# Five PSUM banks for scores and two for transposes in the first batch of attention, instead of four and three

## The chip, the cores and the metric

The kernel runs on one core of one Trainium2 chip. The metric is the device time of one execution in microseconds; the kernel before takes 909.62 us (median of three runs, 909.54 to 909.81).

## The reference

Three layers follow each other. Block-causal attention over 4 batches, 8 heads, 576 positions and 64 channels, in blocks of 64; a feed-forward layer with a squared ReLU; and a mixture of eight experts, of which every token takes one.

```
scores = scale * np.matmul(q, k.transpose(0, 1, 3, 2))
scores = np.where(block_i >= block_j, scores, -1000000000.0)
attn = np.exp(scores - scores.max(-1)); attn = attn / (attn.sum(-1) + 1e-09)
x = np.matmul(attn, v)                     # 2304 tokens x 512
h = np.maximum(x @ w_in, 0.0); x = (s * (h * h) + b) @ w_out
e_idx = np.argmax(x @ w_gate + modality_bias[modality_id], axis=1)
out[mask] = gate_w[mask, None] * (np.maximum(x[mask] @ w1[e], 0.0) @ w2[e])
```

## The kernel before

**Units and steps.** Attention takes two heads at once, a pair, so that 128 partitions are full: four pairs in a batch, sixteen pairs in all. A pair has nine steps, one for each block of 64 query rows; step i has (i + 1) * 64 columns of scores, and the last step is done in two parts of 288 columns. A step passes through these stages (lines of the profile in brackets):

- scores: matmuls into a bank of the pool `sc` [L144 for steps 0 and 1; L147 for the others, three matmuls each, since q and k are split into a high and a low part];
- the row maximum on VectorE (DVE) [L149, and L152 to join the two parts of the last step], then the exponential on ScalarE (ACT), which reads the bank of scores and writes a buffer `p` in SBUF [L154]. The bank of scores is free after it;
- the reciprocal of the row sum on DVE [L163 to L166] and the scaling of p on GpSimd (POOL) [L167];
- the transposes of p on TensorE (PE) into a bank of the pool `tp` [L186], and the copy of that bank to SBUF on ACT [L192], after which the bank is free and so is the buffer p, of which there are six;
- p times v on PE, once for steps 0 to 3 and once for steps 4 to 8, into the bank `o` [L210], copied to `x` by ACT [L212].

**The next pair's q and k.** While a pair is in its steps 4 to 6, q and k of the next pair are turned: four transposes of q into a bank `tw` [L94], which ACT reads four times [L103, L106] and DVE twice for the low part `ql` [L87]; four of k into another bank `tw`, read by ACT twice [L118, L119] and by DVE once [L89, `kl`]; and one for the last 64 rows of both into a bank `te` [L124], read by ACT three times and DVE three times. These banks are of the same pool as those of the p transposes. I call the stretch from the second p times v of one pair to the first exponential of the next pair a pair's boundary; the first batch, with the first step of the second, has three of them, named A, B and C here.

**Banks.** PSUM has eight banks in this kernel. A pool gives out its banks in turn, and a tile waits until all readers of the tile that had its bank before are done. In the first batch (steps 0 to 36 of the program) the pools are `BANKS_0`: scores, transposes, o. After it, `early.close()` and `BANKS_A = (3, 2, 1)`, since the feed-forward layer then takes two banks for work that runs beside attention.

```
LAGS = (1, 5, 7)
NPBUF = 6
BANKS_0 = (4, 3, 1)
BANKS_A = (3, 2, 1)
        if step == per:
            early.close()
            banks.open(c2, tc, 1, *BANKS_A)
```

**What sets the order.** The code is written step by step, with the lags of `LAGS` between a step's stages; a list scheduler in the framework then orders each engine's instructions by its own estimate of when operands and banks are free. So the number of banks also changes the order in which each engine's instructions stand in the program. From step 8 on, weights of the feed-forward layer are converted from 64-bit to 32-bit numbers beside attention [L338 to L340 on DVE, L373 on ACT, L344 on POOL]. The transfers stand in SP's queue [L76, L77 for q, k and v; L329 for the weights].

Of the kernel before, what the change touches and what calls it, by code (L numbers as in the profile page):

```python
# [280 lines left out]
LAGS = (1, 5, 7)  # L281
NPBUF = 6
PTBUF = 1
BANKS_0 = (4, 3, 1)
P_COPY = lambda nc, i: nc.scalar.copy


# [991 lines left out]
def kernel(  # L1279
# [33 lines left out]
    with ExitStack() as c2, ExitStack() as early:  # L1313
        pieces = ffn.beside(c2, range(begun))
        banks = Banks()
        banks.open(early, tc, 0, *BANKS_0)
        plan = [blk for blk in range(begun) for _ in range(NA[blk] + 3)]
# [72 lines left out]
```

## Time and profile before

| | |
|---|---|
| median of three runs | 909.62 us |
| profiled execution, its own time | 911.51 us |
| its span, first to last instruction | 909.9 us |
| mean granted clock of TensorE | 0.992 |
| busy: PE, DVE, ACT, POOL | 878.7, 642.1, 570.0, 218.5 us |

The span's first 62 to 65 us hold the first batch of attention. A matmul's row shows when it started and how long it took until its result was written; since matmuls overlap, a busy PE is not one at its peak. An engine runs its instructions in the program's order, so one that waits holds up all that stand behind it. In a row of the timeline, what stands in square brackets is the idle time of that engine just before the row and who ended it.

### The profile page before, as it was taken

The numbers are of one execution on the slowest core, as the hardware profiler recorded it, in microseconds if no ns is written. First come the engines' busy times: TensorE is split into PE (matmuls) and PEld (weight loads), VectorE is DVE, ScalarE is ACT, GpSimd is POOL, SyncE is SP. The second block draws the span as 40 slices with busy tenths as digits, with TensorE's granted clock in tenths as the row PEclk, the third lists the DMA queues.
The fourth block names the chain that finished last, engine by engine and source line by source line (L and its number), as shares of the span: only waits on it lengthen the run. The fifth ranks groups of instructions, "written<-read, shape, count | busy, mean of one in ns | idle before, by whom it ended". The sixth has DMA issues, their size and how long they took to land. (4 is left out here: it accounts for less than half of the span.)

```text
span 909.9 us, 17059 instructions
## 1 busy us (share of the span) xinstructions
PE 878.7 (97%) x5765; PEld 727.5 (80%) x5765; DVE 642.1 (71%) x1490; ACT 570.0 (63%) x1165; POOL 218.5 (24%) x335
## 2 busy tenths in 40 slices
PE   6889999999999999999999999999999999999996
PEld 5667778888879789999999999998477776776775
DVE  4888996473646445878967777767688887776783
ACT  5888786585757553333565555542287777776773
POOL 4577566133324200000000000002024322222110
PEclk9999999999999999999999999999999999999999
DMA  5666553322221132545212212115345696637500
GB/s 149 162 166 176 148 139 79 98 53 77 62 85 30 49 118 93 162 139 174 59 47 63 76 61 60 47 47 194 110 163 213 230 383 248 223 128 255 189 23 29
DMA packets 109481, 113.84 MB, mean 125 GB/s; under 512 B 62679, under 2 KB 80617, under 8 KB 109387
## 3 DMA queue, kind: packets, MB, share of 16 engines
q1 hardware_dynamic: 105579, 100.74, 35.2%
q0 software_dynamic: 3808, 11.94, 3.8%
q8 instruction: 48, 0.79, 0.4%
q14 instruction: 46, 0.38, 0.1%
HBM read 143.58 MB, written 19.80 MB: 180 GB/s over the span
## 5 line engine op out<-in xcount | busy, mean ns | idle before, releaser
L387 PE MATMUL ph<-xh,wih 128*128 128x256 f32 x576 | 165.7, 288 | 0.1
L387 PE MATMUL ph<-xh,wil 128*128 128x256 f32 x576 | 162.4, 282 | 0.0
L387 PE MATMUL ph<-xl,wih 128*128 128x256 f32 x576 | 162.2, 282 | 0.0
L167 POOL TENSOR_TENSOR p<-p,rc 128x64 f32<-128x64 f32 (+2 forms) x144 | 111.9, 784 | 125.4 <-DVE rc L166 71.4
L387 PEld LDWEIGHTS ph<-xh,wih 128*128 128x128 f32 x576 | 109.1, 189 | 5.2 <-issue 2.9
L387 PEld LDWEIGHTS ph<-xl,wih 128*128 128x128 f32 x576 | 109.2, 190 | 1.3 <-issue 0.2
L387 PEld LDWEIGHTS ph<-xh,wil 128*128 128x128 f32 x576 | 109.2, 190 | 0.6 <-issue 0.4
L149 DVE TENSOR_REDUCE nm<-sc 128x1 f32<-128x288 f32 (+8 forms) x160 | 70.8, 449 | 54.8 <-PE sc L147 47.4
L154 ACT ACTIVATE p<-sc,nm 128x288 f32<-128x288 f32 (+8 forms) x160 | 80.8, 508 | 20.6 <-DVE nm L149 8.7
L1014 DVE TENSOR_TENSOR w1l<-raw,w1h 128x1024 fp32r<-128x1024 f32 x60 | 71.7, 1222 | 22.9 <-ACT w1h L1013 18.7
L1014 DVE TENSOR_TENSOR w2l<-raw,w2h 128x1024 fp32r<-128x1024 f32 x64 | 75.4, 1219 | 10.8 <-ACT w2h L1013 10.6
L1022 POOL DMA_INDIRECT xr<-x_d,gidx_e x2 | 2.3, 1132 | 310.6 <-PE ph L387 310.3
L186 PE MATMUL tp<-ident,p 128*128 128x128 f32 x400 | 66.2, 282 | 5.8 <-POOL p L167 2.5
L1013 ACT CAST w2h<-raw 128x1024 fp32r<-128x1024 f32 x64 | 66.0, 1049 | 7.6 <-PE py L1117 7.1
L397 ACT ACTIVATE r<-ph 128x512 f32<-128x512 f32 x44 | 26.4, 599 | 68.2 <-PE ph L387 68.1
L1013 ACT CAST w1h<-raw 128x1024 fp32r<-128x1024 f32 x60 | 61.6, 1050 | 9.4 <-PE ph L1100 8.7
L192 ACT COPY pt<-tp 128x512 f32<-128x512 f32 (+3 forms) x128 | 61.6, 502 | 7.5 <-PE tp L186 7.0
L398 DVE SCALAR_TENSOR_TENSOR r<-r,sc 128x512 f32<-128x512 f32 x44 | 36.2, 823 | 40.6 <-ACT r L397 40.3
L186 PEld LDWEIGHTS tp<-ident,p 128*128 128x128 f32 x400 | 46.4, 143 | 17.5 <-POOL p L167 6.4
L1117 PE MATMUL py<-w2h,hh 128*128 128x512 f32 x128 | 52.2, 408 | 0.0
L210 PE MATMUL o<-pt,raw_v 128*64 128x320 f32 (+4 forms) x448 | 51.0, 367 | 0.0
L1117 PE MATMUL py<-w2h,hl 128*128 128x512 f32 x128 | 50.8, 397 | 0.0
(306 smaller groups left out, 2272.9 us busy)
## 6 DMA issues: line engine op xcount, KB each, us to landing
raw<-in_moe_w_dram SPq DMA_DIRECT2D x172, 512.0 KB
xr<-xT_d SPq DMA_DIRECT2D x19, 512.0 KB
wr<-in_moe_w_in_dram SPq DMA_DIRECT2D x16, 512.0 KB
wr<-in_moe_w_out_dram SPq DMA_DIRECT2D x16, 512.0 KB
row<-part_d SPq DMA_DIRECT2D x20, 256.0 KB
x_d<-row SPq DMA_DIRECT2D x18, 256.5 KB
xT_d<-x SPq DMA_DIRECT2D x16, 288.0 KB
raw_q<-in_q_dram SPq DMA_DIRECT2D x32, 128.0 KB
```

Of the source, the lines that this page charges most:

```text
L149: ps.last["max"] = nc.vector.tensor_reduce(nm[:, e:e + 1], sc[:, 0:w], AX.X, ALU.max, negate=True)
L154: ps.last["exp"] = nc.scalar.activation(pr[:, k0:k0 + w], scs[e][:, 0:w], AF.Exp, bias=nm[:, 0:1], accum_out=sm[:, e:e + 1])
L167: ps.last["scale"] = nc.gpsimd.tensor_mul(pr[:, 0:n], pr[:, 0:n], rc.to_broadcast([P, n]))
L186: nc.tensor.transpose(t[:, e * P:(e + 1) * P], st[u][i][0][:, c * P:(c + 1) * P], ident)
L192: P_COPY(nc, i0)(o, src)
L210: nc.tensor.matmul(o[r, first * D:n], vt[:, c, hh], p[:, first:, c, r], start=(c == 0), stop=(c == cs[-1]))
L387: nc.tensor.matmul(ph[:, e], self.wi[p][w][:, c, e * P:(e + 1) * P], x[a][:, c], start=(n == 0), stop=(n == 3 * KC - 1))
L397: nc.scalar.activation(r, ph.rearrange("p e (t n) -> p (e t) n", n=P), AF.Relu)
L398: nc.vector.scalar_tensor_tensor(r, r, self.sc[:, 0:1], r, ALU.mult, ALU.mult)
L1013: self.nc.scalar.copy(ws[0][c], r)
L1014: self.nc.vector.tensor_sub(ws[1][c], r, ws[0][c].bitcast(F32))
L1117: nc.tensor.matmul(py, hT[a][:, c], self.w2s[w][c // 2][:, c % 2 * D:c % 2 * D + D], start=(t == 0), stop=(t == 3 * KF - 1))
```

## The change

In the first batch the pool of scores has five banks instead of four and that of transposes two instead of three. Nothing else in the text of the kernel changes.

```
-BANKS_0 = (4, 3, 1)
+BANKS_0 = (5, 2, 1)
```

The scheduler orders the first batch anew; from the second step of the second batch on, the engines' orders agree again. The following pieces are of the program's order, without times. On PE at the start of the program, with the first pair's scores, before the change (the pair in work is the one with kh_171, the next one's q and k are raw_q_207 and raw_k_212):

```order
L144 MATMUL sc_203<-kf_173,qf0_140 128x128
L147 MATMUL sc_224<-kh_171,qh0_136 128x256
L147 MATMUL sc_237<-kh_171,qh0_136 128x256
L94 MATMUL tw_262<-ident_60,raw_q_207 128x128 x4
L147 MATMUL sc_224<-kl_172,qh0_136 128x256
L147 MATMUL sc_224<-kh_171,ql0_138 128x256
L147 MATMUL sc_237<-kl_172,qh0_136 128x256
L147 MATMUL sc_237<-kh_171,ql0_138 128x256
L94 MATMUL tw_289<-ident_60,raw_k_212 128x128 x4
```

And with the change, at the same place:

```order
L144 MATMUL sc_203<-kf_173,qf0_140 128x128
L147 MATMUL sc_224<-kh_171,qh0_136 128x256
L147 MATMUL sc_237<-kh_171,qh0_136 128x256
L147 MATMUL sc_256<-kh_171,qh0_136 128x320
L124 MATMUL te_181<-ident_60,raw_t_149 128x128
L147 MATMUL sc_224<-kl_172,qh0_136 128x256
L147 MATMUL sc_224<-kh_171,ql0_138 128x256
L147 MATMUL sc_237<-kl_172,qh0_136 128x256
L147 MATMUL sc_237<-kh_171,ql0_138 128x256
L147 MATMUL sc_256<-kl_172,qh0_136 128x320
L147 MATMUL sc_256<-kh_171,ql0_138 128x320
L94 MATMUL tw_262<-ident_60,raw_q_207 128x128 x4
```

The next pair's q is now turned after the scores of step 4 instead of before the second matmul of step 2's; a fifth score tile (sc_256) is opened early, and the first pair's tail transposes (te_181) have moved behind it.

On PE at boundary A, before the change (o_554 is the first pair's second p times v, tw_488 and tw_515 are the third pair's q and k, tp_528 the second pair's first p transposes):

```order
L94 MATMUL tw_488<-ident_60,raw_q_337 128x128 x4
L147 MATMUL sc_536<-kh_286,ql1_144 128x448
L147 MATMUL sc_570<-kh_286,qh1_142 128x512
L210 MATMUL o_554<-pt1_383,raw_v_157 64x320 x6
L210 MATMUL o_554<-pt1_383,raw_v_157 64x192 x2
L210 MATMUL o_554<-pt1_383,raw_v_157 64x64 x2
L94 MATMUL tw_515<-ident_60,raw_k_342 128x128 x4
L186 MATMUL tp_528<-ident_60,p_389 128x128
L186 MATMUL tp_528<-ident_60,p_406 128x128
L124 MATMUL te_542<-ident_60,raw_t_338 128x128
```

With the change:

```order
L147 MATMUL sc_570<-kh_286,qh1_142 128x512
L210 MATMUL o_554<-pt1_383,raw_v_157 64x320 x6
L210 MATMUL o_554<-pt1_383,raw_v_157 64x192 x2
L210 MATMUL o_554<-pt1_383,raw_v_157 64x64 x2
L94 MATMUL tw_488<-ident_60,raw_q_337 128x128 x4
L94 MATMUL tw_515<-ident_60,raw_k_342 128x128 x4
L147 MATMUL sc_570<-kl_287,qh1_142 128x512
L147 MATMUL sc_570<-kh_286,ql1_144 128x512
L147 MATMUL sc_608<-kh_286,qh1_142 128x288
L147 MATMUL sc_608<-kl_287,qh1_142 128x288
L147 MATMUL sc_608<-kh_286,ql1_144 128x288
```

The transposes of q have moved from before the p times v to behind it, and those of p (tp_528) from right behind k to behind all scores of the pair's last step and the first of the next pair's (four rows further down, not shown). Boundaries B and C have the same move.

On ACT at boundary A, before the change:

```order
L212 COPY x_417<-o_554 128x320
L118 COPY kf_514<-tw_515 128x128
L119 CAST kh_512<-tw_515 128x512
L192 COPY pt0_527<-tp_528 128x2x128
L154 ACTIVATE p_532,sm_535<-sc_536,nm_534 128x448
```

With the change:

```order
L106 ACTIVATE qh0_136<-tw_488 64x6x64
L118 COPY kf_514<-tw_515 128x128
L119 CAST kh_512<-tw_515 128x512
L154 ACTIVATE p_532,sm_535<-sc_536,nm_534 128x448
L192 COPY pt0_527<-tp_528 128x2x128
```

The reads of the turned q now stand between the copy of o and the reads of the turned k; before they stood ahead of the copy of o. The exponential of step 6 (128x448) needs the buffer p of six steps before, so it waits for the transposes tp_528 in either order.

## Rows read from the trace of the kernel before

**Rows 1.** The page: busy time of each engine; PE's busy tenths in 40 slices.

```profile
PE 878.7 (97%) x5765; PEld 727.5 (80%) x5765; DVE 642.1 (71%) x1490; ACT 570.0 (63%) x1165; POOL 218.5 (24%) x335
PE   6889999999999999999999999999999999999996
```

**Rows 2.** Stretches: length, busy PE, PEld, DVE, ACT, POOL, clock, DMA share, GB/s.

```profile
22.09:36.79 14.70, 12.51 (x93) 9.60 (x92) 12.16 (x41) 13.29 (x46) 7.21 (x16) 1.00 0.79 180
36.79:51.05 14.26, 13.58 (x91) 10.53 (x90) 12.42 (x43) 12.06 (x42) 10.95 (x18) 0.88 0.62 179
51.05:65.10 14.05, 10.71 (x78) 8.11 (x76) 12.43 (x41) 12.30 (x42) 10.23 (x18) 1.00 0.62 160
65.10:81.81 16.71, 15.18 (x100) 11.45 (x102) 13.60 (x43) 13.94 (x46) 10.61 (x19) 0.90 0.57 155
```

**Rows 3.** Timeline of PE and ACT, boundaries A and C: start, us, what.

```profile
26.78 2.28 PE L210 MATMUL o<-pt,raw_v 128*64 128x320 f32 x20
...
56.43 2.28 PE L210 MATMUL o<-pt,raw_v 128*64 128x320 f32 x20
...
27.29 0.47 ACT L106 ACTIVATE qh<-tw 64x384 fp32r<-64x384 f32 x1
...
30.58 0.66 ACT L154 ACTIVATE p<-sc,nm 128x448 f32<-128x448 f32 x1
...
60.24 0.66 ACT L154 ACTIVATE p<-sc,nm 128x448 f32<-128x448 f32 x1
```

**Rows 4.** Timeline of PE, ACT and DVE, 86 to 94 us, banks (3, 2, 1).

```profile
86.65 2.28 PE L210 MATMUL o<-pt,raw_v 128*64 128x320 f32 x20
...
88.97 0.43 ACT L212 COPY x<-o 128x320 f32<-128x320 f32 x1 [0.57 <-PE o L210]
89.55 0.27 ACT L103 ACTIVATE qf<-tw 64x128 f32<-64x128 f32 x1 [0.15 <-PE tw L94]
...
90.38 0.47 ACT L106 ACTIVATE qh<-tw 64x384 fp32r<-64x384 f32 x1
...
92.89 0.64 ACT L154 ACTIVATE p<-sc,nm 128x448 f32<-128x448 f32 x1 [1.25 <-PE tp L186]
...
90.68 0.69 DVE L149 TENSOR_REDUCE nm<-sc 128x1 f32<-128x512 f32 x1 [0.54 <-PE sc L147]
91.29 1.11 DVE L87 SCALAR_TENSOR_TENSOR ql<-tw,qh 64x384 fp32r<-64x384 f32 x2
```

**Rows 5.** Timeline of ACT: last copies before the o of A and C.

```profile
25.16 0.82 ACT L192 COPY pt<-tp 128x512 f32<-128x512 f32 x2
...
54.92 0.76 ACT L192 COPY pt<-tp 128x512 f32<-128x512 f32 x2 [0.17 <-PE tp L186]
```

**Rows 6.** Timeline of DVE and PE, the first pair.

```profile
8.05 0.69 DVE L89 TENSOR_TENSOR kl<-tw,kh 128x512 fp32r<-128x512 f32 x1
...
10.03 1.09 PE L94 MATMUL tw<-ident,raw_q 128*128 128x128 f32 x4 [0.97 <-DMA raw_q<-in_q_dram]
10.77 0.56 PE L147 MATMUL sc<-kl,qh 128*128 128x256 f32 x1
```

**Rows 7.** Behind boundary A: PE and ACT timeline, and a stretch as in rows 2.

```profile
36.46 0.38 PE L147 MATMUL sc<-kh,qh 128*128 128x256 f32 x1 [1.49 <-ACT p L154]
...
40.99 0.76 ACT L192 COPY pt<-tp 128x512 f32<-128x512 f32 x2 [1.16 <-PE tp L186]
...
38.40:42.00 3.60, 3.58 (x16) 3.06 (x16) 3.04 (x10) 2.01 (x7) 3.60 (x4) 0.53 0.16 46
```

**Rows 8.** Behind boundary C: the same views.

```profile
64.13 0.50 ACT L154 ACTIVATE p<-sc,nm 128x288 f32<-128x288 f32 x1 [0.87 <-DVE rc L166]
...
65.56 0.74 PE L144 MATMUL sc<-kf,qf 128*128 128x128 f32 x2 [2.48 <-ACT p L154]
...
65.50:69.00 3.50, 3.44 (x16) 2.51 (x17) 1.90 (x9) 1.87 (x7) 2.17 (x2) 0.52 0.38 112
```

**Rows 9.** Timeline of ACT behind boundary A.

```profile
35.82 0.50 ACT L154 ACTIVATE p<-sc,nm 128x288 f32<-128x288 f32 x1 [0.23 <-DVE rc L165]
```

## The prediction

> **What bounds the kernel now.** I read the page first, then stretches of the first batch, then the timelines of PE, ACT and DVE there. PE is busy 878.7 of 909.9 us, and from the fourth slice of the page's strip to the last but one every slice reads 9 [rows 1]: behind the first batch there is hardly a gap in which a microsecond lost or won early could vanish. The engines' orders agree again from the second batch on, so I carry what the first batch loses or wins to the end one for one.
>
> Inside the first batch PE alone is not the bound. Three stretches run from the first exponential of one pair to that of the next, 14.70, 14.26 and 14.05 us [rows 2]. ACT is busy 13.29, 12.06 and 12.30 of them, which leaves 1.41, 2.20 and 1.75 us; PE is the busier one in the second, where its clock stands at 0.88. So a pair is a chain over PE, ACT and DVE with ACT nearest to full: what makes ACT wait, and is not made up by a wait that ACT would have had anyway, lengthens the pair.
>
> **The change part by part.** It adds, removes and lengthens no instruction. It moves them, and changes who waits for a bank.
>
> *The boundaries (loss).* With three transpose banks the scheduler turns the next pair's q before the second p times v, and ACT reads it while PE does these 20 matmuls: the last read of q starts at 27.29 under the matmuls of 26.78 + 2.28 [rows 3]. With two banks both are held by the last p transposes until their copies are made, so q comes behind the p times v, the new order on PE says. Then a chain stands open: p times v, copy of o, four reads of q on ACT, two `ql` on DVE, and only then is a bank free for the next p transposes, for which the step-6 exponential waits because it needs their buffer p. Queued behind that exponential on ACT are the copy of those transposes, the tail's reads and all further exponentials.
>
> The trace of before has this very order once, where the banks are (3, 2, 1) [rows 4]: p times v starts at 86.65, copy of o at 88.97, q from 89.55 to 90.85, `ql` from 91.29, and the exponential at 92.89 after a wait of 1.25 us: 6.24 us from start to exponential. Boundaries A and C have 30.58 - 26.78 = 3.80 and 60.24 - 56.43 = 3.81 [rows 3]. The difference is 2.43 us. Of it 0.44 is a row maximum that held DVE until 91.29 while q was ready at 90.85 [rows 4], and need not stand there: 1.99 to 2.43.
>
> Against it, p times v can start sooner, since the transposes of q no longer stand ahead of it: its last operand is copied at 25.16 + 0.82 = 25.98 and 54.92 + 0.76 = 55.68, and it started 0.80 and 0.75 us later [rows 3, 5]. The gain is 0 to 0.80; I take 0.75, as the new order has only score matmuls there. Net per boundary: 1.99 - 0.80 = 1.2 at least, 2.43 at most; I take (1.99 + 2.43) / 2 - 0.75 = 1.45. What covers some of it: at C ACT waited 0.87 us for DVE before the last step's exponential [rows 8], at A 0.23 [rows 9]; a later ACT finds that work done. A, B, C: 1.22 + 1.45 + 0.58 = 3.25 us. The ends are 3 x 1.2 - 1.1 = 2.5 and 3 x 2.43 - 1.1 = 6.2.
>
> *The first pair (gain).* Before, PE stood 0.97 us at the transposes of the second pair's q, whose transfer landed late, and scores that could use `kl` from 8.05 + 0.69 = 8.74 on started at 10.77 [rows 6]. Now scores come first and q is turned when it is there. The gain is at least 0 (ACT and DVE may set the pace) and at most 10.77 - 8.74 = 2.03; I take the wait itself, 0.97.
>
> *The fifth score bank (gain).* Behind boundary A PE waited 1.49 us for a bank of scores that an exponential had to free, and then ran 3.6 us at a granted clock of 0.53, near the lower level of 1.2 GHz; ACT waited 1.16 us there for the slow transposes [rows 7]. With five banks this score tile takes the bank of the step before, so this wait goes. At most that gives 1.49 and half of 3.58, together 3.3 us; at least nothing, if the clock falls there again. What is late next is the bank of transposes, and PE's idle time at the boundary grows. I take half of ACT's own wait, 0.6.
>
> *The clock at B (loss).* Both low spells, 0.53 and 0.52, come behind a standstill of PE of 1.49 and 2.48 us [rows 7, 8]; the boundary B has neither now. With the chain above PE stands still at B too. The cost is 0 to half of 3.58, 1.8 us; as ACT sets most of the pace I take 0.6.
>
> *At no cost:* at the change of pools the first tile of the new score pool waits, in either order, for the same exponential, so the wait of 2.48 us [rows 8] stays; the moved tail transposes lie in it. On SP one or two transfers of weights pass those of q, which is turned later by the length of the p times v.
>
> Sum: 3.25 - 0.97 - 0.6 + 0.6 = +2.3 us. On the profiled execution's own time of 911.51 this is 913.8 (span 909.9 to 912.2). The median of the runs is 1.89 below that execution, so the forecast is 909.62 + 2.3 = 911.9 us.
>
> **The rivals.** *The fifth bank wins (faster).* If PE's scores, not ACT's chain, set the pace, the first pair gives its 2.03 and boundary A its 3.3, 5.3 in all, against boundaries at their lower end, 2.5: -2.8 us, 906.8 us. The point from which it decides is a boundary that costs under 5.3 / 3 = 1.8 us each together with gains at their upper ends. For it: PE did wait for score banks, 1.49 and 2.48 us. Against it: the longer of these two stays, and ACT is busy 85 to 90% of a pair.
>
> *They cancel (no change).* With the boundaries at 2.5 and the gains at 0.97 and ACT's full 1.16, no new spell at B: +0.4, 910.0 us. For it: the pair behind the change of pools, with only two transpose banks, took 16.71 us, but with ACT idle for only 2.77 of it and a clock of 0.90 in it [rows 2], so two banks need not cost much in themselves.
>
> *The clock falls at every boundary (slower still).* Each standstill brings a spell at half clock, and boundary A is not relieved: 3.25 - 0.97 + 1.8 = +4.1, 913.7 us. For it: both longest waits of PE in these stretches were followed by one. Against it: behind the first standstill it took 1.9 us of normal running before the clock fell, so not each need bring one. The Trainium skill bears on this (TensorE: Matmul & The Clock Gate, section A second HAM failure mode: psum-queue depth-cycling): where groups of matmuls go round through few PSUM banks, PE idles shortly between them, its clock swings between the levels, and throughput is lost although single matmuls look normal. By that rule the time is this rival's; the two spells of rows 7 and 8 agree with it, the stretch from 51.05 to 65.10 with clock 1.00 shows no case of it.
>
> **How the numbers follow.** What a measurement of this kernel can tell from no change is 0.2%, 1.8 us. I give the forecast 0.40, the half clock at every boundary 0.18, cancelling 0.28 and the faster rival 0.14. So slower by over 0.2% is 0.58, within 0.2% is 0.28, faster 0.14. The boundary term decides: it has a row of this kernel for its size, while the gains are waits that may turn into others. The range for 8 in 10 is 908.4 to 914.8: it leaves out most of the faster rival, and reaches past the half-clock rival by 1.1 us because the boundary may cost up to 2.43 each. The forecast's own range is 911.4 to 913.2.
>
> **What would show it.** Right, if in the changed profile the step-6 exponential stands 5.2 to 6.3 us behind the start of the second p times v at A, B and C with a wait for `tp` just ahead of it; if PE's wait of 0.97 for raw_q and that of 1.49 for a score bank are gone; if a stretch with a clock near 0.5 stands behind B; and if the first exponential of the fifth pair, 65.10 before, comes at about 67.4. Wrong, if that exponential comes at or before 65.1: then the boundaries cost less than I took, or ACT's waits elsewhere shrank more. Also wrong, if it is late and the end is not: then the rest of the program has slack that I deny it.

## The result and the profile after

With five banks for scores and two for transposes the kernel takes 915.60 us (median of four runs, 915.12 to 916.16), against 909.61 us before in the same job: a ratio of 1.0063, with a 95% interval of 1.0050 to 1.0075. It is slower by 6.0 us by the medians. The forecast was 911.9, with a range up to 914.8: the direction was right, and the size was less than half of what came. The profiled execution of after took 916.16 us (span 914.5, mean granted clock 0.986); that of before 911.51 (span 909.9, clock 0.992), so the two traces differ by 4.65 us.

The page of after: busy time of each engine, and in 40 slices PE's busy tenths and the granted clock in tenths [rows 1].

```profile
PE 882.9 (97%) x5765; PEld 730.7 (80%) x5765; DVE 639.9 (70%) x1490; ACT 570.5 (62%) x1165; POOL 218.5 (24%) x335
...
PE   6978999999999999999999999999999999999996
...
PEclk9988999999999999999999999999999999999999
```

Counts are unchanged, PE is busy 4.2 us longer, and the third and fourth slice (46 to 91 us) show a clock below 9 tenths, where before had 9 in every slice.

The first exponential of the second, the fourth and the fifth pair, from the timeline of ACT (start, us, what):

```profile
20.71 0.36 ACT L154 ACTIVATE p<-sc,nm 128x64 f32<-128x64 f32 x1
...
52.78 0.36 ACT L154 ACTIVATE p<-sc,nm 128x64 f32<-128x64 f32 x1
...
69.75 0.36 ACT L154 ACTIVATE p<-sc,nm 128x64 f32<-128x64 f32 x1
```

And the stretches from one to the next, with columns as in [rows 2]; the second begins at the third pair's, 37.87:

```profile
20.71:37.87 17.16, 15.41 (x108) 11.70 (x105) 12.79 (x44) 12.64 (x43) 8.54 (x17) 0.94 0.78 201
37.87:52.78 14.91, 12.08 (x79) 8.98 (x79) 12.28 (x43) 12.31 (x43) 8.74 (x15) 0.91 0.58 153
52.78:69.75 16.97, 14.60 (x88) 11.32 (x84) 11.60 (x41) 12.79 (x42) 10.79 (x18) 0.80 0.47 126
```

Before they took 14.70, 14.26 and 14.05 us. After starts 1.38 us ahead (20.71 against 22.09) and then loses 2.46, 0.65 and 2.92 us. At the fifth pair, forecast for 67.4, it is 69.75 - 65.10 = 4.65 us late, and the span ends 4.6 us late: between these two traces, what the first batch lost went to the end one for one. The clock column, 0.94, 0.91 and 0.80 instead of 1.00, 0.88 and 1.00, is the part that the prediction had too small.

The boundaries A and B in the timelines of PE, ACT and DVE (columns as in [rows 3, 4]):

```profile
26.39 2.28 PE L210 MATMUL o<-pt,raw_v 128*64 128x320 f32 x20
...
32.05 0.41 PE L186 MATMUL tp<-ident,p 128*128 128x128 f32 x2 [0.68 <-DVE ql L87]
...
28.71 0.43 ACT L212 COPY x<-o 128x320 f32<-128x320 f32 x1 [0.72 <-PE o L210]
29.29 0.27 ACT L103 ACTIVATE qf<-tw 64x128 f32<-64x128 f32 x1 [0.15 <-PE tw L94]
...
32.39 0.64 ACT L154 ACTIVATE p<-sc,nm 128x448 f32<-128x448 f32 x1 [1.02 <-PE tp L186]
...
30.79 1.11 DVE L87 SCALAR_TENSOR_TENSOR ql<-tw,qh 64x384 fp32r<-64x384 f32 x2
...
42.50 2.27 PE L210 MATMUL o<-pt,raw_v 128*64 128x320 f32 x20
...
47.05 0.43 PE L144 MATMUL sc<-kf,qf 128*128 128x64 f32 x2 [0.85 <-ACT kf L118]
48.01 0.41 PE L186 MATMUL tp<-ident,p 128*128 128x128 f32 x2 [0.53 <-DVE ql L87]
...
52.22 1.55 PE L210 MATMUL o<-pt,raw_v 128*64 128x256 f32 x8
```

This is the chain as forecast: p times v at 26.39, copy of o at 28.71, q read from 29.29 on, `ql` until 31.90, the transposes at 32.05 and the exponential at 32.39, 6.00 us behind the start. At B it is 48.34 - 42.50 = 5.84, at C 65.84 - 59.99 = 5.85. The last row is the new thing: at B the next p times v of eight matmuls takes 1.55 us; at full clock, behind A at 35.67, it takes 0.87.

### The profile page after: what moved, and what is told of

Same layout as the page of the kernel before. It is cut to its first block, busy times and chain, and to the rows that moved or that the text cites. A ratio compares the mean times of both kernels' runs of the same rounds, so it can differ in the third digit from the quotient of the medians.

```text
span 914.5 us, 17060 instructions
## 1 busy us (share of the span) xinstructions
PE 882.9 (97%) x5765; PEld 730.7 (80%) x5765; DVE 639.9 (70%) x1490; ACT 570.5 (62%) x1165; POOL 218.5 (24%) x335
## 5 line engine op out<-in xcount | busy, mean ns | idle before, releaser
L186 PE MATMUL tp<-ident,p 128*128 128x128 f32 x400 | 68.4, 289 | 7.5 <-DVE ql L87 2.5
L1117 PE MATMUL py<-w2h,hl 128*128 128x512 f32 x128 | 50.8, 397 | 0.0
```

The lines of the kernel that those rows point to most:

```text
L186: nc.tensor.transpose(t[:, e * P:(e + 1) * P], st[u][i][0][:, c * P:(c + 1) * P], ident)
L1117: nc.tensor.matmul(py, hT[a][:, c], self.w2s[w][c // 2][:, c % 2 * D:c % 2 * D + D], start=(t == 0), stop=(t == 3 * KF - 1))
```

## The experiments

The theories. **Theory 1:** the loss comes from the lost third transpose bank, which puts the next pair's q behind p times v; **1a:** its price is the chain over ACT up to the step-6 exponential. **Theory 2:** its price is rather the half clock that follows PE's standstills. **Theory 3:** the fifth score bank or the new order costs by itself. A stretch at about half the granted clock is called a spell below. Each kernel was run 5 to 12 times, beside the kernel before in the same job (medians of before 909.59, 910.34 and 909.60 us in the jobs of e1 to e4, e5 to e8 and e9 to e12), and each ratio is against before of its own job.

**Two transpose banks alone (e1_421).**

```
-BANKS_0 = (5, 2, 1)
+BANKS_0 = (4, 2, 1)
```

> Two banks for transposes as in the changed kernel, but four for scores as before; the eighth bank lies idle. Theory 1 (the third transpose bank is what is lost: q is turned behind p times v, the step-6 exponential comes 5.8 to 6.0 us behind its start, and PE's standstills there bring spells at half clock): as slow as the changed kernel or slower, 914 to 917 us. Theory 3 (the fifth score bank and the earlier scores that it allows are what costs): as before, 909 to 911 us.

Measured: 914.92 us, ratio 1.0069 (1.0052 to 1.0087). Theory 1 holds; at A the exponential stands 6.24 us behind p times v, a little more than expected. In its trace the fifth pair's first exponential is at 69.69, against 69.75 with five score banks: the fifth bank gives nothing, and costs nothing, that these figures show.

**Eight buffers p, with the change and without it (e2_521_p8, e3_431_p8).**

```
-NPBUF = 6
+NPBUF = 8
```

> The changed kernel with eight buffers p instead of six, so that the step-6 exponential needs no transposes of six steps before. Theory 1a (the chain over ACT to that exponential is the main cost, 1.0 us of wait in each of four places): 3 to 4 us are won back, 911.5 to 912.5 us, and the clock spells shrink since scores' banks come free sooner. Theory 2 (the half clock behind each boundary is the main cost, and it hangs on PE's standstills for kf and ql, which stay): at most 2 us are won, 913.5 to 915.5 us, with stretches of granted clock near 0.5 behind the same boundaries.

> Control: the kernel before with eight buffers p. Its step-6 exponentials come 3.8 us behind the second p times v and wait little, so all theories give 908.5 to 910.5 us.

Measured: 907.72 us, ratio 0.9983 (0.9968 to 0.9998), with banks (5, 2, 1); 907.70 us, ratio 0.9984 (0.9973 to 0.9995), with (4, 3, 1). Both sizes were missed: the control won 1.9 us too, and with the change 7.9 us came back, twice what theory 1a gave. But the comparison is clear: with eight buffers the two splits of the banks take the same time, within intervals of 1.0 to 1.4 us either way. ACT at boundary A of e2_521_p8:

```profile
25.88 0.63 ACT L154 ACTIVATE p<-sc,nm 128x448 f32<-128x448 f32 x1
...
27.19 0.43 ACT L212 COPY x<-o 128x320 f32<-128x320 f32 x1 [0.59 <-PE o L210]
...
31.23 0.37 ACT L192 COPY pt<-tp 128x256 f32<-128x256 f32 x1 [0.19 <-PE tp L186]
```

q still stands behind p times v (24.87), but the step-6 exponential now runs under it, at 25.88 instead of 6 us behind. The granted clock of this trace is 1.00 in all of the first batch. So with eight buffers the new order costs nothing in the total. Inside the first batch it still costs something. From the second pair's first exponential to the fifth's, with banks (5, 2, 1) and then with (4, 3, 1), columns as in [rows 2]:

```profile
20.56:64.42 43.86, 36.88 (x260) 27.37 (x258) 36.98 (x123) 38.01 (x125) 28.14 (x50) 1.00 0.69 181
```

```profile
22.00:63.93 41.93, 34.81 (x257) 26.86 (x255) 36.65 (x124) 37.31 (x124) 28.03 (x50) 1.00 0.73 185
```

Both are at full clock, and the new order is 1.93 us longer; its start, 1.44 us earlier, hides most of that. The traces of after and of this kernel end 10.0 us apart (914.5 and 904.5), of which 69.75 - 64.42 = 5.3 lie in the first batch. The rest lies behind it, where the control gained too.

**A bank for q alone (e4_q_bank).** Line 94 takes its bank for q from a pool of its own.

```
-BANKS_0 = (5, 2, 1)
+BANKS_0 = (4, 2, 1)
+        if ph == 0:
+            self.f = ctx.enter_context(tc.tile_pool(name="a0_ps_f", bufs=1, space=PSUM, reuse_waits="tile"))
-        t = ps.t.tile([P, 512], F32, name="tw", tag="t")
+        pool = ps.f if own and ps.f else ps.t
+        t = pool.tile([P, 512], F32, name="tw", tag="t")
```

> Four banks for scores, two for transposes, and the eighth bank for the next pair's turned q alone. Theory 1 (what is lost is q turned ahead of p times v): the order of before comes back at the boundaries, the step-6 exponential 3.8 to 4.5 us behind the start of p times v, 908.5 to 911 us. Rival (it is the transposes of p themselves that need three banks): 913 us or more, with ACT waits for tp in the middle of pairs.

Measured: 906.52 us, ratio 0.9967 (0.9955 to 0.9978); faster than expected, and than both kernels. The exponential stands 3.80 us behind p times v at A, B and C. Two banks are enough for p, k and the tails, if q has one that these don't hold.

**q one step earlier (e5_521_q_early).**

```
-                    if i == 4:
+                    if i == (3 if u < 4 else 4):
```

> The changed kernel (banks 5, 2, 1; six buffers p), with the next pair's q turned one step earlier in the first batch, so that the program's order has it ahead of the second p times v again. Theory 1 (the loss is q turned behind p times v, which opens the chain to the step-6 exponential): at least two thirds of the 6 us come back, 908 to 911.5 us, the exponential 4 to 4.8 us behind the start of p times v, and no spell at half clock behind B. Rival (two banks for transposes are too few by themselves, whatever the order): 914 to 916 us.

Measured: 909.80 us, ratio 0.9995 (0.9983 to 1.0007): all of the loss is gone with the banks still at (5, 2, 1). Boundary B in the timelines of PE and ACT:

```profile
41.78 2.16 PE L210 MATMUL o<-pt,raw_v 128*64 128x320 f32 x16 [0.48 <-ACT pt L192]
...
39.97 0.49 ACT L106 ACTIVATE qh<-tw 64x384 fp32r<-64x384 f32 x1
...
45.85 0.68 ACT L154 ACTIVATE p<-sc,nm 128x448 f32<-128x448 f32 x1
```

q is read at 39.97, before p times v, and the exponential comes 4.07 us behind it, without a wait. This is the cleanest test of theory 1, and its rival fell. No spell stands behind B (1.00 from 45 to 55 us); one stands behind A instead (0.72 from 32 to 38 us), so the earlier q does not remove every spell.

**Repeated matmuls in PE's standstill (e6_521_fill4, e7_521_fill8, e10_521_fill3), beside the changed kernel once more (e9_521_again).** The step-0 score matmul of the four boundaries is done 5, 9 and 4 times; the order of all other rows is unchanged.

```
-                scored[0] = nc.tensor.matmul(
+                for _ in range(5 if i == 0 and u in (1, 2, 3, 4) else 1): scored[0] = nc.tensor.matmul(
```

> The changed kernel, whose step-0 score matmuls are done five times instead of once at the four boundaries (same result, no new wait, order of all engines unchanged otherwise), so that TensorE works in part of its wait for ql. Theory 2 (the half clock that follows these standstills is the larger part of the loss): the spells shrink or go, and the time falls by 2 to 4 us, to 911.5 to 913.5 us. Theory 1a (the chain over ACT is the larger part, the half clock lies under ACT's waits): 914.5 to 916.5 us even where the clock stays up.

> The same with nine of these matmuls instead of one, which covers the whole wait for ql (0.5 to 0.7 us) and may overrun it by some tenths at each boundary. Theory 2: as or below the kernel with five, 911 to 913.5 us, and no stretch near half clock behind A, B or C. Theory 1a: 915 to 917.5 us.

> The changed kernel once more, beside the one with repeated matmuls on the same chip, to size what the repeats win. All theories: 914.5 to 916.5 us.

> The changed kernel with the step-0 score matmuls of the four boundaries done four times, in the same order. If the spells of half clock behind the first pair's boundary and behind B stay away as with five, the time is 1.7 us (by medians of two jobs) to 3.4 us (by the first batch of two traces) below the changed kernel of this job; if four are too few, the spells are back and it is within 0.5 us of it.

Measured: 913.91 us (ratio 1.0044, 1.0031 to 1.0057) with five, 914.00 us (1.0046, 1.0032 to 1.0060) with nine; in another job 913.30 us (1.0039, 1.0026 to 1.0052) with four and 913.71 us (1.0043, 1.0028 to 1.0058; runs from 911.98 to 916.03) for the unchanged after, less than I had expected. With five, in stretches of columns as in [rows 2]:

```profile
16.00:24.00 8.00, 7.07 (x55) 5.89 (x55) 5.90 (x27) 6.69 (x25) 5.49 (x12) 1.00 0.67 184
46.00:54.00 8.00, 6.93 (x52) 5.75 (x53) 6.34 (x25) 6.93 (x24) 5.15 (x10) 1.00 0.75 172
```

And the exponential at its boundary B, from the timeline of ACT:

```profile
47.46 0.63 ACT L154 ACTIVATE p<-sc,nm 128x448 f32<-128x448 f32 x1 [1.05 <-PE tp L186]
```

The spells behind the first pair's boundary and behind B are gone in this trace, while the chain is whole: 47.46 - 41.43 = 6.03 us. Its fifth pair begins at 66.34, so between this trace and that of after the spells make 69.75 - 66.34 = 3.4 us. The trace with four is a closer match to after: the same start (20.70), the same chain (6.01, 5.84 and 5.84 us), a clock of 1.00 from there to 62 us, and the fifth pair at 65.64, which makes the spells 4.1 us:

```profile
20.70:65.64 44.94, 39.73 (x280) 30.75 (x279) 37.04 (x126) 37.47 (x123) 27.98 (x50) 0.97 0.67 178
```

The medians don't confirm this size. The repeats win 1.7 us against the first job and 0.4 us beside after on one chip, which the intervals can't tell from nothing. So the expectation for four failed: the spells stayed away in the execution that left a trace, but the median is not 1.7 to 3.4 us lower; the eight executions range from 911.60 to 915.82 us, with clocks of 0.992 down to 0.987. Nine matmuls, also at 1.00 from the second pair to the fifth, came out between the two theories' ranges. They took 2.22 us, not some tenths more than the wait but 0.9, which I had mis-sized; they lengthen the chain to 6.93 us.

The unchanged after was thus 1.9 us faster in the later job. The times of its eleven executions go with the clock: the four with a mean of 0.990 or 0.991 took 911.98 to 913.71 us, the seven with 0.984 to 0.988 took 915.12 to 916.16. All four of the first job were of the latter. So luck has a part in the miss: the later job's 913.71 lies inside the forecast's range, the first job's 915.60 outside it. Before shows the same on a smaller scale: of 62 executions in the three jobs, the 35 at 0.992 have a median of 910.60, the 12 at 0.996 one of 908.82 us.

**Seven buffers p (e11_521_p7).** NPBUF = 7, banks (5, 2, 1).

> The changed kernel with seven buffers p. Now the exponential of step 7, not of step 6, needs the buffer that the first p transposes of the pair free; it comes about half a microsecond of ACT work later. Theory 1a: ACT has the step-6 exponential to do under p times v, its wait for tp falls from 1.0 to below 0.6 us per boundary, and 3 us or more come back: 909 to 912.5 us. Rival (what helped with eight buffers was something else, in the later batches, where the control with banks 4, 3, 1 won 1.9 us too): 913 us or more.

Measured: 910.58 us, ratio 1.0007 (0.9998 to 1.0016). ACT's waits, from the second pair's first exponential to the fifth's (us in total, times, longest), of after and then of this kernel:

```profile
ACT x L212 <- PE o L210: 3.7, 4, 1.5
ACT pt L192 <- PE tp L186: 3.5, 3, 1.5
ACT p L154 <- PE tp L186: 2.7, 3, 1.0
```

```profile
ACT p L154 <- PE tp L186: 2.6, 3, 0.9
...
ACT x L212 <- issue: 1.0, 1, 1.0
ACT x L212 <- PE o L210: 0.5, 2, 0.4
...
ACT pt L192 <- PE tp L186: 0.2, 1, 0.2
```

The time came as theory 1a had it, but not by the wait it named: the wait for tp did not shorten, it moved to the step-7 exponential (47.12 at B, 0.86 us). Two other waits went. Those before the copy of o, 3.7 us in after, are 0.5 here and one of 1.0 for which the profile shows no releaser, since ACT has the step-6 exponential to do meanwhile. And the copies' waits for p transposes fell from 3.5 to 0.2 us; the two longest of after (1.51 before 22.68 and 1.41 before 54.64) lie in its spells, and this trace has no spell before 64 us:

```profile
20.84:64.82 43.98, 36.99 (x261) 27.51 (x261) 37.04 (x123) 37.80 (x125) 27.25 (x50) 1.00 0.71 185
```

This stretch takes 43.98 us, against 44.94 with six buffers and four repeated matmuls (its last 3 us at half clock) and 49.04 in after. So in the traces the seventh buffer is worth at most about 1 us by itself, and the other 4 go with the spells: there theory 2 has the larger part of the price, theory 1a the smaller. The medians of the repeated matmuls leave these shares open.

**The opposite move (e12_341).** BANKS_0 = (3, 4, 1).

> The opposite move: three banks for scores, four for transposes. Theory 1: q and k of the next pair are turned well ahead of p times v and the step-6 exponential stands at most 3.8 us behind it; the lost score bank costs only where PE waited for one (1.49 us behind A). 907.5 to 911 us. Theory 3 (banks for scores are what the first batch lacks): 912 us or more.

Measured: 914.68 us, ratio 1.0050 (1.0037 to 1.0063). My expectation failed: its boundaries are short (2.39, 3.34 and 4.11 us, the last over the 3.8 expected), and yet it is as slow as after. PE's waits from 22.8 to 69.3 us:

```profile
PE sc L144 <- ACT p L154: 3.9, 3, 1.6
PE tp L186 <- POOL p L167: 1.8, 4, 0.9
```

PE waits 3.9 us for a score bank. Behind the last of these waits (1.50 us before 50.11) the clock is 0.50 from 52 to 58 us, and the second pair begins 0.72 us later than in before (22.81 against 22.09). So (3, 4, 1) is 5 us slower than (4, 3, 1); the parts of the waits, the spell, the later start and the fourth transpose bank in it are not separated. A step from four to five score banks gives nothing (e1_421).

**A version (e8_q_bank_p8).** The bank for q and eight buffers p together.

> A version: four banks for scores, two for transposes, one for the next pair's q alone, and eight buffers p. If what each part won alone adds up (3.1 and 1.9 us below the kernel before), 904.6 us; if both remove the same wait, 906 to 907.7 us.

Measured: 906.44 us, ratio 0.9958 (0.9944 to 0.9973). Below before of its own job that is 3.9 us, against 3.1 for the bank for q alone, with intervals that overlap. The two gains don't add up to 5.0, as expected if both parts remove the same wait.

## Why the prediction was half right

**The boundaries: right.** Each was to cost 1.99 to 2.43 us in the distance from p times v to exponential. With five matmuls, where no spell of half clock disturbs A, B and C, that distance is 6.03 us at each, against 3.80 and 3.81: +2.22. p times v stood 0.52, 1.07 and 0.86 us closer to the pair's first exponential (forecast 0.75), and from the step-6 exponential to the next pair 0.73, 0.33 and 0.95 us were covered (forecast 0.23 and 0.87 for A and C). Net 6.67 - 2.45 - 2.01 = 2.2 us. The forecast had 3.25 for them and 0.6 less for the score bank at A, which lies in the 1.07: 2.65. With four matmuls the same stretch gives 44.94 - 43.01 = 1.9 us.

**The first pair: right in place.** The wait of 0.97 for raw_q is gone [rows 6]; scores that use `kl` start at 9.38, and the gain is 1.38 in after and 0.97 in e6_521_fill4. I had not listed that the first pair has a boundary too (its exponential waits 1.04 us for `tp` at 16.80); its cost lies in the stretch behind it, the first of the spells below.

**The fifth bank: right that its wait goes, and no more.** The wait of 1.49 and the spell behind A [rows 7] are gone in this trace, but e1_421 shows that four banks do the same: the new order took the wait away, not the fifth bank. The wait of 2.48 us at the change of pools [rows 8], which was to stay, is 0.48 in after (before 70.25): other work of PE now stands before it.

**The clock: the step that failed.** "The clock at B (loss)" was put at 0.6 us, 1.8 at most, and at B alone. After has half clock in three places, in stretches of columns as in [rows 2]:

```profile
18.50:22.50 4.00, 3.47 (x18) 2.48 (x18) 1.51 (x11) 2.67 (x10) 3.31 (x6) 0.61 0.71 232
50.50:57.00 6.50, 6.23 (x30) 5.30 (x31) 3.41 (x14) 5.09 (x18) 3.64 (x8) 0.51 0.68 168
66.00:74.00 8.00, 6.50 (x29) 4.66 (x30) 4.13 (x20) 6.28 (x22) 5.72 (x10) 0.57 0.75 203
```

That is behind the first pair's boundary, behind B and, longer than before, behind C; none behind A. The 6.5 us at 0.51 are near the lower level of 1.2 GHz, and nearly twice the 3.6 us of [rows 7] that I had taken as the upper end. The spells make 3.4 us between the two traces named above, 4.1 by the trace with four matmuls, and 2.6 us between the medians of the two groups of after's executions (913.0 and 915.6). The rival "the clock falls at every boundary" had the mechanism, with 0.18, and at 1.8 us it was too small as well.

**From the traces to the medians.** 1.24 us without these spells and 3.4 for them make the 4.65 of the traces (0.54 and 4.11 by the trace with four matmuls). The medians differ by 6.0, since the profiled execution of before lay 1.9 us over its median and that of after 0.6. One place of that is seen: both of these traces fall to half clock once more, far behind the first batch (after from 690 to 700 us, at 0.83; before in the first row), and e1_421's does not (second):

```profile
680.00:690.00 10.00, 8.23 (x32) 6.33 (x31) 10.00 (x12) 8.41 (x13) 8.49 (x3) 0.84 0.80 309
```

```profile
680.00:690.00 10.00, 8.23 (x45) 6.63 (x44) 10.00 (x12) 10.00 (x14) 4.67 (x2) 1.00 0.98 376
```

Whether the faster executions of before have this spell is not recorded. Relative to before, e1_421 is 4.59 us late at the fifth pair and 2.2 at the end. I carried the difference of one execution over to a median of executions whose spells differ. Which spells an execution gets, and why all four of after's first job had low clocks, stays open, since only one execution of a run leaves a trace. The second trace of after, that of e9_521_again, has a spell behind A that the first has not; its fifth pair begins at 70.08, 0.33 us later, and its span ends 0.9 us sooner.

## What to carry to other kernels

Count banks by what holds them at the moment of need: the transposes that open the next pair found both banks held by the last pair's, and the price was a chain over three engines, which an earlier issue (e5_521_q_early), a bank of its own (e4_q_bank) or one more buffer behind the waiting instruction (e11_521_p7) each made up for. When a change adds standstills of half a microsecond to the busiest engine, allow for a spell of half clock behind each of them, as long as the longest and not a typical one, and compare kernels over executions, not over one trace each.

## What was unexpected of the hardware

The half clock came behind standstills of PE of 0.5 to 0.9 us that follow each other within some microseconds (at B 0.85, 0.53, 0.27 and 0.67 us from 46.2 to 50.8), not only behind single ones of 1.5 and 2.5 us as before; and not behind every such group (A had 0.68, 0.27 and 0.52 us and kept 1.00 in after, while the trace of e9_521_again has half clock there, 0.50 from 36 to 40 us). The same program took 905.82 to 911.99 us over twelve executions of e2_521_p8, with mean granted clocks of 0.998 down to 0.991. The Trainium skill (TensorE: Matmul & The Clock Gate, section A second HAM failure mode: psum-queue depth-cycling) ties swings of the clock between its levels to short idle stretches of PE between groups of matmuls that cycle through PSUM banks; it names no number of banks. The trace of after agrees, with short standstills around two transpose banks. Before's two spells came behind single standstills of 1.49 and 2.48 us instead, and with eight buffers p the same two banks ran the first batch at 1.00, though PE stood still there for up to 1.18 us (before 64.90).
